# Last stage of a chained retention, hard-swish and SoLU kernel: word copies on ScalarE, the first pair's sums moved to the preceding block, output units within the last pair

## The chip, the cores and the metric

The kernel runs on one core of a Trainium2 chip. The metric is the device time of one execution in microseconds. Engines: TensorE (PE, with PEld for its weight loads), VectorE (DVE), ScalarE (ACT), GpSimd (POOL), and SyncE (SP), whose queue issues nearly all DMA transfers.

## The reference

```python
ret = (scale * q @ k.T * Dmat) @ v                 # 4 x 8 heads, 576 positions, 64 wide
x   = ret, heads side by side                      # 2304 tokens x 512
h   = x @ w_in                                     # 512 -> 2048
x   = (h * clip(h + 3, 0, 6) / 6) @ w_out          # 2048 -> 512: "x2" below
h   = x @ w_in2                                    # 512 -> 1024
e   = exp(h - max(h)); sm = e / (sum(e) + 1e-9)
s   = h * sm                                       # SoLU
ln  = (s - mean(s)) / sqrt(var(s) + 1e-6) * g_ln
out = ln @ w_out2                                  # 1024 -> 512
```

All in float32. The kernel keeps that accuracy by holding each matrix as two parts, a rounded one and the rest ("split": ScalarE copies the rounded part, GpSimd or VectorE subtracts it), and multiplying three times: high by high, high by low, low by high.

## The kernel before

The 2304 tokens are five blocks, four of 512 and block 4 of 256. A first stage computes the retention and, for the first six feed-forward groups of 128, a part of x2. Stage B goes over the blocks in the order `B_ORDER` = 3, 0, 1, 2, 4 and does the other ten groups: a first layer (`mlp_hs`: 40 steps of three matmuls each, four to a group; after each group ScalarE r, VectorE gf, ScalarE g, GpSimd g) and a second layer (`mlp_x2s`: 40 steps), whose sums `evac_full` adds to the earlier part and stores in DRAM as `x2f`. Beside stage B the second network's weights are prepared in 16 steps (`w2q`; ScalarE three activations each, VectorE, stores `w2s`), at the steps that `STEPS_B` lists for blocks 0, 1 and 2; their raw parts come by SP into two buffers `wraw`.

The last stage goes over nine pairs of 128-token tiles in the order `C_ORDER`, two pairs to a block of 512. The first product is a Strassen form: `load_x2` fetches a pair's x2 (`x2r`), `forms_x2` makes four sums on GpSimd and splits four operands into `xt` tiles (`his` on ScalarE, `los` on GpSimd), and `product` does seven products p = 0 to 6, each six matmuls, of prepared weight forms `w2t` (named b11, b21, t2, t1, b22, t3, t4 in that order). They are written in the groups (0,1), (2,3), (4,5), (6); a group's two banks are of a ring of two, so product 4 waits until the banks of products 0 and 1 have been read, product 6 until those of 2 and 3.

For each of the two tiles r of a pair VectorE then sums (`total`, `add_u`) with ScalarE's `first_u`, ScalarE takes `exp`, VectorE multiplies (`weigh`), ScalarE squares (`square`), GpSimd takes the power of the variance (`power`), VectorE normalizes (`norm`). The result must be transposed for the next product. The DMA engines transpose only 2-byte words, so `half_out` copies the lower (w = 0) and upper (w = 1) 16-bit words of each float apart into `lh`, an SP transfer transposes each into `lhT`, and `half_in` puts them together again in `lT` (w = 0 on VectorE, w = 1 on ScalarE). `split_hi` (ScalarE) and `split_lo` (GpSimd) make the two parts `lt` in a ring of four half tiles. `mm_out` is the output product: eight units of three matmuls for a tile, then ScalarE copies `osb` and SP stores it.

The order within each engine of the last stage is written out by hand. `at(when, fn)` notes an instruction with a planned time, `fill(n_small, n_out)` puts n_small steps of block 4's second layer (planned 0.36 us each) and n_out output units (0.68 us each) between the groups of products, and everything is emitted in order of planned time to engines that keep the order of the program. So a planned time only says which instruction stands behind which. Stage B isn't pinned in that way, save its weight steps; there a planner orders by its own costs. Output units begin in pair 2, four after each group; the last pair has none, and the remaining 56 follow it in one run. In pairs 0 and 1 the steps of block 4's second layer take their place.

Before block 4, pairs 0 and 1 (of block 2, the block just finished) are loaded; pair 0's forms are made inside block 4's first layer:

```python
load_x2(0)
load_x2(1)
...
for i, _ in enumerate(mlp_hs(t, FB, g4, g_4)):
    if i == 6:
        for step in chain(*forms_x2(0)):
            step()
```

Of the kernel before, what the change touches and what calls it, by code (L numbers as in the profile page):

```python
# [10 lines left out]
F32R = mybir.dt.float32r  # L11
# [3 lines left out]
ACTF = mybir.ActivationFunctionType  # L15
# [15 lines left out]
RELOAD = (0, 1, 2)  # L31
X2_LAG = 3
B_ORDER = (3, 0, 1, 2, 4)
C_ORDER = (2, 3, 0, 1, 4)
NX = 8
STEPS_B = ((6, 20, 42, 50, 58, 66), (6, 20, 42, 50, 58, 66), (6, 20, 42, 50))
W_FROM = 2
A_FROM = 4
AHEAD = 2
# [33 lines left out]
def retention_hardswish_solu_kernel(ctx, tc, kt, qt, kn, vt, w1, w2i, w2o, gln, decay, place, out):  # L73
# [580 lines left out]
    for i, _ in enumerate(first_b):  # L654
# [2 lines left out]
        j = i - NP * (len(FB) - X2_LAG)  # L657
        if 0 <= j < NP:
            xb[B_ORDER[1], j] = load_x(B_ORDER[1], j)
    w2q = Weights(w2_halves(pb), True)  # L660
    w2q.load_to(2)
    for k, t in enumerate(B_ORDER[1:-1]):
        after = B_ORDER[k + 2]
        for i, _ in enumerate(part_b(t)):
            if i in STEPS_B[k]:
                w2q.step()
            j = i - (4 * len(FB) + 4)
            if after in RELOAD and j >= 0 and j % 4 == 0 and j < 4 * NP:
                xb[after, j // 4] = load_x(after, j // 4)


    pairs = [(t, c) for t in C_ORDER for c in range(BLOCKS[t][1] // 256)]
    tiles = [BLOCKS[t][0] + 256 * c + 128 * i for t, c in pairs for i in range(2)]
    last = len(pairs) - 1
    xt = [p0.tile([128, 2, 512], F32R, tag="x", bufs=NX, name=f"xt{k}") for k in range(NX)]
    x2r, x2w, h2, ebuf, stats, us, lnT, turned, lTs = {}, {}, {}, {}, {}, {}, {}, {}, {}
    banks, raw_bufs = {}, []

    def load_x2(i):

# [11 lines left out]
    def forms_x2(i):  # L692

        lo, hi = x2r.pop(i)
        (a11, a21), (a12, a22) = (
            [x.rearrange("p k (t c) -> p t k c", c=128)[:, t] for t in range(2)] for x in (lo, hi)
        )
        s12, s34 = (pb.tile([128, 2, 2, 128], F32, tag="xraw", bufs=2, name=f"{n}_{i}") for n in ("s12", "s34"))
        xa = xt[6].rearrange("p a (i k c) -> p a i k c", i=2, k=2)[:, :, i % 2]
        x2, x12, x34 = xt[3 * (i % 2):3 * (i % 2) + 3]  # L700
        sums = [
            lambda o=o, a=a, b=b, op=op: ge.tensor_tensor(out=o, in0=a, in1=b, op=op) for o, a, b, op in (
                (s12[:, 0], a21, a22, ALU.add), (s12[:, 1], s12[:, 0], a11, ALU.subtract),
                (s34[:, 0], a11, a21, ALU.subtract), (s34[:, 1], a12, s12[:, 1], ALU.subtract),
            )
        ]
        splits = (
            (xa[:, 0], xa[:, 1], a11), (x2[:, 0], x2[:, 1], hi.rearrange("p k n -> p (k n)")),
            (x12[:, 0], x12[:, 1], s12.rearrange("p s k c -> p (s k c)")),
            (x34[:, 0], x34[:, 1], s34.rearrange("p s k c -> p (s k c)")),  # L710
        )
        his = [lambda a=a, v=v: se.activation(out=a, in_=v, func=ACTF.Copy) for a, _, v in splits]
        los = [
            lambda a=a, b=b, v=v: ge.tensor_tensor(out=b, in0=v, in1=f32(a), op=ALU.subtract) for a, b, v in splits
        ]
        x2w[i] = {
            name: [[x[:, a, at + k * step:at + k * step + 128] for a in range(2)] for k in range(2)]
            for name, x, at, step in (
                ("a11", xt[6], 256 * (i % 2), 128), ("a12", x2, 0, 256), ("a22", x2, 128, 256),
                ("s1", x12, 0, 128), ("s2", x12, 256, 128), ("s3", x34, 0, 128), ("s4", x34, 256, 128),  # L720
            )
        }
        return sums, his, los

    def product(i, p):

# [72 lines left out]
    def half_out(i, r, w):  # L799

        words = ebuf[i, r].rearrange("p a b -> p (a b)").bitcast(U16).rearrange("p (n w) -> p w n", w=2)
        if w == 0:
            turned[i, r] = p0.tile([128, 2, 8, 128], U16, tag="wraw", bufs=WRAW, name=f"lhT{i}_{r}")
        part = p0.tile([128, 1024], U16, tag=("wz", "wt")[w], bufs=2, name=f"lh{i}_{r}_{w}")
        ve.tensor_copy(out=part, in_=words[:, w])
        sy.dma_start(out=turned[i, r][:, w], in_=part, transpose=True)

    def half_in(i, r, w):
# [38 lines left out]
    t = B_ORDER[-1]  # L847
    load_x2p(t, 0)
    load_x2p(t, 1)
    load_x2(0)  # L850
    load_x2(1)
    g4, held = {}, []

    def g_4(ff):
# [5 lines left out]

    to_load = {18: ("b11", "wbi"), 22: ("b21", "wbi"), 28: ("t2", "wi"), 36: ("t1", "wi")}
    for i, _ in enumerate(mlp_hs(t, FB, g4, g_4)):
        if i == 6:
            for step in chain(*forms_x2(0)):
                step()
        if i in to_load:
            w2_load(*to_load[i])

# [39 lines left out]
    for i in range(last + 1):  # L908
        starts.append(now)
        for group in GROUPS:  # L910
            for p in group:
                at(now, product, i, p)
                now += 2 * UNIT
                ends[i, p] = now
            fill(5 if i == 0 else 4, 4 if 2 <= i < last else 0)
    fill(0, out_left)

    def spread(i, n, offsets):
# [8 lines left out]

    for i in range(last + 1):
        e = [ends[i, p] for p in range(7)]
        for when, fn, *args in (  # L930
            (e[0] + 0.2, first_u), (e[1] + 0.6, total, 0, 0, 2, 1), (e[2] + 0.1, add_u, 2, 2),
            (e[3] + 0.1, add_u, 4, 3), (e[4] + 0.1, total, 0, 1, 4, 4), (e[4] + 0.8, top, 0), (e[4] + 1.0, exp, 0),
# [7 lines left out]
            (e[4] + 16.8, split_hi, 0, 0), (e[4] + 17.4, split_hi, 0, 1),  # L940
            (e[4] + 17.5, split_lo, 0, 0), (e[4] + 18.8, split_lo, 0, 1),
            (e[6] + 14.0, half_in, 1, 0), (e[6] + 14.1, half_in, 1, 1),
            (e[6] + 23.5, split_hi, 1, 0), (e[6] + 24.1, split_hi, 1, 1),
            (e[6] + 24.2, split_lo, 1, 0), (e[6] + 25.5, split_lo, 1, 1),
        ):
            at(when, fn, i, *args)
        if i + 2 <= last:
# [62 lines left out]
```

## Time and profile before

| | us |
|---|---|
| runs shown (3) | 675.83, 678.3, 679.1 |
| median | 678.3 |
| the profiled execution | 678.33 |
| its span, first to last instruction | 676.5 |

| engine | busy us | share of the span | instructions |
|---|---|---|---|
| TensorE | 657.2 | 97% | 3914 |
| VectorE | 350.2 | 52% | 606 |
| ScalarE | 357.2 | 53% | 651 |
| GpSimd | 329.8 | 49% | 342 |

The shares are means over stages with different limits: VectorE's 52% is below 30% in some stretches and near 90% in the last stage. A matmul's end is modelled in the trace, so a busy TensorE may hide short pauses; the starts of runs of matmuls tell more. Planned engines keep their order, so an instruction can be late because the one ahead of it waits.

### The profile page before, as it was taken

The numbers are of one execution on the slowest core, as the hardware profiler recorded it, in microseconds if no ns is written. First come the engines' busy times: TensorE is split into PE (matmuls) and PEld (weight loads), VectorE is DVE, ScalarE is ACT, GpSimd is POOL, SyncE is SP. The second block draws the span as 40 slices with busy tenths as digits, with TensorE's granted clock in tenths as the row PEclk, the third lists the DMA queues.
The fourth block names the chain that finished last, engine by engine and source line by source line (L and its number), as shares of the span: only waits on it lengthen the run. The fifth ranks groups of instructions, "written<-read, shape, count | busy, mean of one in ns | idle before, by whom it ended". The sixth has DMA issues, their size and how long they took to land.

```text
span 676.5 us, 10633 instructions
## 1 busy us (share of the span) xinstructions
PE 657.2 (97%) x3914; PEld 545.0 (81%) x3914; DVE 350.2 (52%) x606; ACT 357.2 (53%) x651; POOL 329.8 (49%) x342
## 2 busy tenths in 40 slices
PE   9989999999999999999999999999999999999797
PEld 6778888887889888888888888898878777777587
DVE  1645445217213454244474344122888798889760
ACT  5878846346425665264364255043565665655453
POOL 4676744024222434145043033048796998888353
PEclk9999999999999999999999999999999999999799
DMA  9979727158206162558854732479683443343332
GB/s 319 303 257 329 262 72 240 47 165 324 88 32 187 50 200 84 156 167 284 321 171 157 247 126 78 140 268 354 129 230 91 97 111 81 96 104 78 79 73 83
DMA packets 80312, 112.92 MB, mean 167 GB/s; under 512 B 42626, under 2 KB 48002, under 8 KB 80260
## 3 DMA queue, kind: packets, MB, share of 16 engines
q1 hardware_dynamic: 80112, 112.22, 52.9%
q8 instruction: 31, 0.51, 0.3%
q14 instruction: 21, 0.17, 0.1%
q10 hardware_dynamic: 148, 0.01, 0.0%
HBM read 70.80 MB, written 31.98 MB: 152 GB/s over the span
## 4 chain that ended last, share of the span: by engine, by line
PE 65%; DVE 10%; POOL 7%; DMA 7%; ACT 6%; issue 4%; SPq 0%; ACTq 0%; POOLq 0%; DVEq 0%
PE h L260 25%; PE x L283 17%; PE acc L283 8%; PE o L69 5%; PE h L69 3%; DVE h L69 3%; PE xp L385 3%; POOL lt L69 2%; DVE lh L69 2%; ACT e L69 2%; DMA wraw<-in_w_dram 2%; POOL stat L69 2%; PE s L385 1%; PE x L69 1%; DVE e L69 1%
## 5 line engine op out<-in xcount | busy, mean ns | idle before, releaser
L277 POOL TENSOR_TENSOR g<-gf,g 128x512 fp32r<-128x512 f32 (+1 forms) x78 | 95.6, 1227 | 225.6 <-ACT g L276 215.9
L283 PE MATMUL x<-g,w 128*128 128x512 f32 x576 | 132.4, 389 | 0.1
L260 PE MATMUL h<-xb,w 128*128 128x512 f32 (+1 forms) x600 | 129.5, 359 | 1.0 <-DVE gf L271 1.0
L283 PEld LDWEIGHTS x<-g,w 128*128 128x128 f32 x576 | 108.0, 188 | 23.3 <-POOL g L277 0.5
L271 DVE SCALAR_TENSOR_TENSOR gf<-r,h 128x512 f32<-128x512 f32 (+1 forms) x80 | 50.6, 633 | 130.9 <-ACT r L270 105.5
L260 PEld LDWEIGHTS h<-xb,w 128*128 128x128 f32 x600 | 98.6, 189 | 17.1 <-DVE gf L271 1.2
L69 PE MATMUL o<-w,lt 128*128 128x512 f32 (+1 forms) x456 | 102.9, 378 | 1.6 <-DMA w<-w2s 1.6
L69 PEld LDWEIGHTS o<-w,lt 128*128 128x128 f32 x456 | 82.3, 188 | 18.4 <-DMA w<-w2s 2.4
L270 ACT ACTIVATE r<-h,half 128x512 f32<-128x512 f32 (+1 forms) x80 | 50.8, 638 | 61.6 <-PE h L260 61.5
L260 PE MATMUL h<-xB,w 128*128 128x512 f32 x360 | 82.4, 389 | 0.0
L260 PEld LDWEIGHTS h<-xB,w 128*128 128x128 f32 x360 | 67.6, 188 | 14.0
L69 POOL TENSOR_TENSOR lt<-lT,lt 128x512 fp32r<-128x512 f32 x36 | 58.4, 1639 | 22.6 <-ACT lt L69 12.2
L276 ACT ACTIVATE g<-gf 128x512 fp32r<-128x512 f32 (+1 forms) x78 | 46.0, 590 | 43.8 <-DVE gf L271 42.2
L69 ACT ACTIVATE e<-h,stat 128x1024 f32<-128x1024 f32 x36 | 41.2, 1145 | 39.4 <-DVE stat L69 39.4
L283 PE MATMUL acc<-g,w 128*128 128x512 f32 (+1 forms) x264 | 61.8, 360 | 0.0
L69 PE MATMUL h<-w2t,xt 128*128 128x512 f32 x216 | 55.5, 401 | 2.9 <-DVE h L69 2.9
L283 PEld LDWEIGHTS acc<-g,w 128*128 128x128 f32 x264 | 46.9, 188 | 8.7
L69 PEld LDWEIGHTS h<-w2t,xt 128*128 128x128 f32 x216 | 41.0, 193 | 13.6 <-DVE h L69 5.0
L141 DVE TENSOR_SCALAR wz<-wz 128x512 int32<-128x512 int32 x44 | 28.5, 649 | 40.0 <-ACT wz L133 39.9
L69 PE MATMUL h<-w2b,xt 128*128 128x512 f32 x162 | 41.7, 403 | 4.6 <-DVE stat L69 4.4
L69 DVE COPY lh<-e 128x1024 uint16<-128x1024 uint16 x36 | 42.8, 1211 | 0.2
L69 PEld LDWEIGHTS h<-w2b,xt 128*128 128x128 f32 x162 | 30.5, 193 | 12.7 <-DVE stat L69 6.7
(113 smaller groups left out, 850.8 us busy)
## 6 DMA issues: line engine op xcount, KB each, us to landing
wraw<-in_w_dram SPq DMA_DIRECT2D x32, 512.0 KB, 5.0
xs<-xb SPq DMA_DIRECT2D x12, 512.0 KB, 5.9
xB<-xs SPq DMA_DIRECT2D x12, 512.0 KB, 6.5
rv<-in_vt_dram SPq DMA_DIRECT2D x16, 288.0 KB, 5.7
x2l<-x2s SPq DMA_DIRECT2D x18, 256.0 KB, 4.0
x2r<-x2f SPq DMA_DIRECT2D x9, 512.0 KB, 4.4
out_dram<-osb SPq DMA_DIRECT2D x17, 256.0 KB, 2.1
x2s<-x2p SPq DMA_DIRECT2D x16, 256.0 KB, 2.7
```

The costliest lines, as they stand in the source:

```text
L69: return lambda *args, **kw: self.keep(op(*args, **kw))
L141: ve.tensor_scalar(out=z, in0=z, scalar1=3, scalar2=None, op0=ALU.logical_shift_left)
L260: nc.tensor.matmul(hp, w1t[ff, 0][:, a, c], xb[t, p][:, b, :n], start=(p == 0 and i == 0), stop=(p == NP - 1 and i == 2),)
L270: se.activation(out=r, in_=hp, func=ACTF.Relu, scale=1.0 / 6.0, bias=half)
L271: ve.scalar_tensor_tensor(out=gf, in0=r, scalar=1.0, in1=hp, op0=ALU.min, op1=ALU.mult)
L276: se.activation(out=g[ff][:, 0], in_=gf, func=ACTF.Copy)
L277: ge.tensor_tensor(out=g[ff][:, 1], in0=gf, in1=f32(g[ff][:, 0]), op=ALU.subtract)
L283: te.matmul(acc, w1t[ff, 1][:, a, c], g[:, b], start=(first and i == 0), stop=(last and i == 2))
L385: keep(nc.tensor.matmul(*args, **kw))
```

## The change

Five edits, all for the last stage or just ahead of it.

1. `C_ORDER` begins with block 3, whose x2 is stored long before. The loads of pairs 0 and 1 and pair 0's `forms_x2` go into `before_c`, called at steps 41, 42 and 52 of block 2's stage B (1, 2 and 12 of its second layer). The `xt` tiles are taken there, and renumbered so that pair 0's lie in slots that were block 1's.
2. The four weight steps of block 2 go from its steps 6, 20, 42, 50 to 4, 12, 20, 28, all in the first layer.
3. `half_out` copies the upper words on ScalarE instead of VectorE.
4. Two output units follow each group of the last pair.
5. The last tile's splits are planned 18.0 us after the pair's last product instead of 23.5.

```diff
@@ -31,9 +31,9 @@
 RELOAD = (0, 1, 2)
 X2_LAG = 3
 B_ORDER = (3, 0, 1, 2, 4)
-C_ORDER = (2, 3, 0, 1, 4)
+C_ORDER = (3, 0, 1, 2, 4)
 NX = 8
-STEPS_B = ((6, 20, 42, 50, 58, 66), (6, 20, 42, 50, 58, 66), (6, 20, 42, 50))
+STEPS_B = ((6, 20, 42, 50, 58, 66), (6, 20, 42, 50, 58, 66), (4, 12, 20, 28))
 W_FROM = 2
 A_FROM = 4
 AHEAD = 2
@@ -657,24 +657,11 @@
         j = i - NP * (len(FB) - X2_LAG)
         if 0 <= j < NP:
             xb[B_ORDER[1], j] = load_x(B_ORDER[1], j)
-    w2q = Weights(w2_halves(pb), True)
-    w2q.load_to(2)
-    for k, t in enumerate(B_ORDER[1:-1]):
-        after = B_ORDER[k + 2]
-        for i, _ in enumerate(part_b(t)):
-            if i in STEPS_B[k]:
-                w2q.step()
-            j = i - (4 * len(FB) + 4)
-            if after in RELOAD and j >= 0 and j % 4 == 0 and j < 4 * NP:
-                xb[after, j // 4] = load_x(after, j // 4)
-
-
     pairs = [(t, c) for t in C_ORDER for c in range(BLOCKS[t][1] // 256)]
     tiles = [BLOCKS[t][0] + 256 * c + 128 * i for t, c in pairs for i in range(2)]
     last = len(pairs) - 1
-    xt = [p0.tile([128, 2, 512], F32R, tag="x", bufs=NX, name=f"xt{k}") for k in range(NX)]
     x2r, x2w, h2, ebuf, stats, us, lnT, turned, lTs = {}, {}, {}, {}, {}, {}, {}, {}, {}
-    banks, raw_bufs = {}, []
+    banks, raw_bufs, xt = {}, [], []
 
     def load_x2(i):
 
@@ -696,8 +683,8 @@
             [x.rearrange("p k (t c) -> p t k c", c=128)[:, t] for t in range(2)] for x in (lo, hi)
         )
         s12, s34 = (pb.tile([128, 2, 2, 128], F32, tag="xraw", bufs=2, name=f"{n}_{i}") for n in ("s12", "s34"))
-        xa = xt[6].rearrange("p a (i k c) -> p a i k c", i=2, k=2)[:, :, i % 2]
-        x2, x12, x34 = xt[3 * (i % 2):3 * (i % 2) + 3]
+        xa = xt[3].rearrange("p a (i k c) -> p a i k c", i=2, k=2)[:, :, i % 2]
+        x2, x12, x34 = xt[4 * (i % 2):4 * (i % 2) + 3]
         sums = [
             lambda o=o, a=a, b=b, op=op: ge.tensor_tensor(out=o, in0=a, in1=b, op=op) for o, a, b, op in (
                 (s12[:, 0], a21, a22, ALU.add), (s12[:, 1], s12[:, 0], a11, ALU.subtract),
@@ -716,11 +703,36 @@
         x2w[i] = {
             name: [[x[:, a, at + k * step:at + k * step + 128] for a in range(2)] for k in range(2)]
             for name, x, at, step in (
-                ("a11", xt[6], 256 * (i % 2), 128), ("a12", x2, 0, 256), ("a22", x2, 128, 256),
+                ("a11", xt[3], 256 * (i % 2), 128), ("a12", x2, 0, 256), ("a22", x2, 128, 256),
                 ("s1", x12, 0, 128), ("s2", x12, 256, 128), ("s3", x34, 0, 128), ("s4", x34, 256, 128),
             )
         }
         return sums, his, los
+
+    def before_c(i):
+
+        if i == 1:
+            xt.extend(p0.tile([128, 2, 512], F32R, tag="x", bufs=NX, name=f"xt{k}") for k in range(NX))
+            load_x2(0)
+        elif i == 2:
+            load_x2(1)
+        elif i == 12:
+            for step in chain(*forms_x2(0)):
+                step()
+
+    w2q = Weights(w2_halves(pb), True)
+    w2q.load_to(2)
+    for k, t in enumerate(B_ORDER[1:-1]):
+        after = B_ORDER[k + 2]
+        for i, _ in enumerate(part_b(t)):
+            if i in STEPS_B[k]:
+                w2q.step()
+            if t == B_ORDER[-2]:
+                before_c(i - 4 * len(FB))
+            j = i - (4 * len(FB) + 4)
+            if after in RELOAD and j >= 0 and j % 4 == 0 and j < 4 * NP:
+                xb[after, j // 4] = load_x(after, j // 4)
+
 
     def product(i, p):
 
@@ -802,7 +814,10 @@
         if w == 0:
             turned[i, r] = p0.tile([128, 2, 8, 128], U16, tag="wraw", bufs=WRAW, name=f"lhT{i}_{r}")
         part = p0.tile([128, 1024], U16, tag=("wz", "wt")[w], bufs=2, name=f"lh{i}_{r}_{w}")
-        ve.tensor_copy(out=part, in_=words[:, w])
+        if w:
+            se.activation(out=part, in_=words[:, w], func=ACTF.Copy)
+        else:
+            ve.tensor_copy(out=part, in_=words[:, w])
         sy.dma_start(out=turned[i, r][:, w], in_=part, transpose=True)
 
     def half_in(i, r, w):
@@ -847,8 +862,6 @@
     t = B_ORDER[-1]
     load_x2p(t, 0)
     load_x2p(t, 1)
-    load_x2(0)
-    load_x2(1)
     g4, held = {}, []
 
     def g_4(ff):
@@ -860,9 +873,6 @@
 
     to_load = {18: ("b11", "wbi"), 22: ("b21", "wbi"), 28: ("t2", "wi"), 36: ("t1", "wi")}
     for i, _ in enumerate(mlp_hs(t, FB, g4, g_4)):
-        if i == 6:
-            for step in chain(*forms_x2(0)):
-                step()
         if i in to_load:
             w2_load(*to_load[i])
 
@@ -912,7 +922,7 @@
                 at(now, product, i, p)
                 now += 2 * UNIT
                 ends[i, p] = now
-            fill(5 if i == 0 else 4, 4 if 2 <= i < last else 0)
+            fill(5 if i == 0 else 4, 0 if i < 2 else 4 if i < last else 2)
     fill(0, out_left)
 
     def spread(i, n, offsets):
@@ -927,6 +937,7 @@
 
     for i in range(last + 1):
         e = [ends[i, p] for p in range(7)]
+        late = e[6] + (23.5 if i < last else 18.0)
         for when, fn, *args in (
             (e[0] + 0.2, first_u), (e[1] + 0.6, total, 0, 0, 2, 1), (e[2] + 0.1, add_u, 2, 2),
             (e[3] + 0.1, add_u, 4, 3), (e[4] + 0.1, total, 0, 1, 4, 4), (e[4] + 0.8, top, 0), (e[4] + 1.0, exp, 0),
@@ -940,8 +951,8 @@
             (e[4] + 16.8, split_hi, 0, 0), (e[4] + 17.4, split_hi, 0, 1),
             (e[4] + 17.5, split_lo, 0, 0), (e[4] + 18.8, split_lo, 0, 1),
             (e[6] + 14.0, half_in, 1, 0), (e[6] + 14.1, half_in, 1, 1),
-            (e[6] + 23.5, split_hi, 1, 0), (e[6] + 24.1, split_hi, 1, 1),
-            (e[6] + 24.2, split_lo, 1, 0), (e[6] + 25.5, split_lo, 1, 1),
+            (late, split_hi, 1, 0), (late + 0.6, split_hi, 1, 1),
+            (late + 0.7, split_lo, 1, 0), (late + 2.0, split_lo, 1, 1),
         ):
             at(when, fn, i, *args)
         if i + 2 <= last:
```

## Rows read from the trace of the kernel before

**Rows 1.** Busy us of each engine by stretch (x instructions), granted clock, DMA

```profile
388.00:415.00 27.00, 27.00 (x121) 22.36 (x120) 11.67 (x16) 14.88 (x24) 10.71 (x9) 1.00 0.36 121
...
415.00:442.30 27.30, 27.30 (x123) 22.62 (x122) 6.96 (x10) 5.01 (x8) 2.27 (x2) 1.00 0.31 97
...
583.94:605.47 21.53, 21.00 (x92) 16.75 (x91) 19.23 (x31) 12.88 (x23) 18.65 (x19) 1.00 0.41 98
...
627.03:640.05 13.02, 8.59 (x26) 6.52 (x25) 10.62 (x20) 4.79 (x10) 4.87 (x5) 0.74 0.49 102
```

**Rows 2.** Chain that ended last, in order of time: start, us, tile

```profile
387.89 27.20 PE h L260 x120
...
530.83 3.13 DMA lhT<-lh
```

**Rows 3.** TensorE, block 4 and pairs 0 to 3: start, us, operation, tiles

```profile
442.13 13.11 PE L260 MATMUL h<-xb,w 128*128 128x256 f32 x108
...
460.34 2.91 PE L69 MATMUL h<-w2b,xt 128*128 128x512 f32 x12
...
515.09 2.88 PE L69 MATMUL h<-w2b,xt 128*128 128x512 f32 x12
```

**Rows 4.** TensorE from pair 6 on [idle <-releaser]

```profile
597.16 1.65 PE L69 MATMUL h<-w2t,xt 128*128 128x512 f32 x6 [0.48 <-DVE h L69]
...
622.91 2.89 PE L69 MATMUL h<-w2b,xt 128*128 128x512 f32 x12
...
632.99 2.93 PE L69 MATMUL h<-w2b,xt 128*128 128x512 f32 x6 [4.43 <-DVE stat L69]
...
639.89 33.14 PE L69 MATMUL o<-w,lt 128*128 128x512 f32 x168
```

**Rows 5.** GpSimd (POOL) in block 4's first layer and in a steady pair

```profile
453.72 1.30 POOL L714 TENSOR_TENSOR xt<-x2r,xt 128x512 fp32r<-128x512 f32 x1
...
585.76 3.97 POOL L69 TENSOR_TENSOR lt<-lT,lt 128x512 fp32r<-128x512 f32 x2
...
599.35 2.55 POOL L69 TENSOR_TENSOR lt<-lT,lt 128x512 fp32r<-128x512 f32 x2
```

**Rows 6.** VectorE (DVE) in a steady pair and at the end

```profile
588.62 1.66 DVE L69 COPY lh<-e 128x1024 uint16<-128x1024 uint16 x1
...
592.52 2.26 DVE L69 COPY lh<-e 128x1024 uint16<-128x1024 uint16 x2
...
634.63 0.69 DVE L69 COPY lh<-e 128x1024 uint16<-128x1024 uint16 x1
...
641.93 1.22 DVE L69 SCALAR_TENSOR_TENSOR h<-h,e 128x1024 f32<-128x1024 f32 x1
```

**Rows 7.** Waits of TensorE from 440 us on: total us, times, longest

```profile
PE o L69 <- DMA w<-w2s: 1.6, 2, 1.2
...
PE h L260 <- DVE gf L271: 1.0, 1, 1.0
...
PE x L69 <- DVE gf L271: 0.9, 1, 0.9
```

**Rows 8.** The queue of SyncE (SP): DMA issues in order of time

```profile
498.27 1.09 SPq L69 DMA_DIRECT2D w<-w2s  x2
```

**Rows 9.** Groups of ScalarE, 540.87 to 605.47 us: busy, mean ns | idle

```profile
L69 ACT ACTIVATE e<-h,stat 128x1024 f32<-128x1024 f32 x13 | 14.9, 1144 | 12.4 <-DVE stat L69 12.4
...
L69 ACT ACTIVATE lT<-lhT 128x1024 uint16<-128x1024 uint16 x6 | 8.3, 1376 | 0.0
...
L69 ACT ACTIVATE lt<-lT 128x512 fp32r<-128x512 f32 x12 | 6.9, 621 | 4.9 <-DVE lT L69 4.9
```

**Rows 10.** ScalarE (ACT) in a steady pair and in the last pair

```profile
593.11 0.64 ACT L69 ACTIVATE xt<-s 128x512 fp32r<-128x512 f32 x1 [2.87 <-POOL s L69]
...
630.42 0.58 ACT L69 ACTIVATE h<-h 128x512 f32<-128x512 f32 x1
...
645.55 0.63 ACT L69 ACTIVATE lt<-lT 128x512 fp32r<-128x512 f32 x1 [2.03 <-PE o L69]
```

## The prediction

> **What bounds the kernel now.** I read the busy time by stretch first, to see which engine sets the time in which stage. Up to the end of block 2 TensorE has no gap: its two layers take 27 us each with ScalarE, VectorE and GpSimd far from full [rows 1]. The chain that ended last gives the price of one 512-column matmul there: 27.20 us / 120 = 0.2267 us [rows 2]. A steady pair of the last stage needs 42 of these for its products and 48 for its 16 output units: 90 x 0.2267 = 20.40 us. It takes more: pair 3 begins at 515.09 [rows 3] and pair 8, the last, at S = 622.91 [rows 4], so five pairs take 107.82 us, 21.56 each. The missing 1.16 us are short pauses ahead of products 4 and 6 behind VectorE, as the 0.48 us at 597.16 and the slow refill behind it [rows 4].
>
> The other engines' rows of a steady pair say why: VectorE is busy 19.23 of 21.53 us, GpSimd 18.65, ScalarE only 12.88 [rows 1]. The chain in order of time runs in that stage through GpSimd, VectorE and ScalarE and never through TensorE. Its round, from one split of output words to the next: GpSimd's two subtractions (585.76, 3.97 us) [rows 5], the power of the row's variance, VectorE's norm, its two copies of words (592.52, 2.26) [rows 6], an addition, a word put back, then ScalarE's splits, its own word, exp, VectorE's weighing, ScalarE's square, GpSimd again. So the pairs are bound by a round of queues of about 21.5 us, with TensorE 1.16 us below it.
>
> Outside the steady pairs TensorE waits in three places. In block 4's first layer and its first accumulation it stands 1.0 and 0.9 us [rows 7], because GpSimd has the sums and splits of pair 0's x2 in front of block 4's g (one is at 453.72) [rows 5]. In pair 2 it waits 1.6 us, in two parts, for the last output weights [rows 7], whose transfers SP issues only at 498.27 [rows 8]. In the last pair, which has no output units between its products, it waits 4.43 us ahead of product 4 [rows 4], and the granted clock of that stretch is 0.74 in the mean [rows 1]: the engine had stood still, and the next matmuls ran at 1.2 instead of 2.4 GHz. From S the products and the 168 matmuls left end at 639.89 + 33.14 = 673.03 = S + 50.1; the work is 42 x 0.2267 + 33.1 = 42.6, so 7.5 us are lost there, 4.4 by waiting and 3.1 by the clock.
>
> **The change part by part.**
>
> *Pair 0 first from block 3.* Its load and its twelve sums and splits go to block 2's second layer, where ScalarE is busy 5.01 and GpSimd 2.27 of 27.3 us and TensorE doesn't wait for either [rows 1]; the slots of xt0 to xt3 were block 1's. Hidden there at no cost; were the cover gone, the 1.9 us of block 4 would come back. In block 4 GpSimd then has only g. From 442.13 to 460.34 TensorE does 132 matmuls of 256 columns; at 13.11 / 108 = 0.1214 each that is 16.0 instead of 18.2 us. **Gain 2.2** (at least the two waits, 1.9; if the planner puts the forms back beside block 4, nothing). Two x2r loads leave SP's burst at block 4's start for block 2's second layer, behind nothing there that waits (block 3's x2 was stored two blocks before); no matmul waits for that burst, so I count nothing.
>
> *The last weight steps earlier.* Two of four steps go from the second to the first layer of block 2. A step has three ScalarE activations, about as long as a split of 621 ns [rows 9], so 4 us more beside 14.88 of 27.0 [rows 1], with their two raw loads and two stores on SP in the same 27 us. TensorE has four banks ahead of ScalarE. At no cost; uncovered it would be those 4 us.
>
> *Upper words by ScalarE.* Two copies per pair leave VectorE: 1.66 us (row 0) and half of 2.26 (row 1), 2.8 together, because each collides with GpSimd; the same copy alone takes 0.69 [rows 6]. ScalarE's copy isn't in the trace, but the way back is, same size and with the stride on the other side: 1376 ns [rows 9]. I take 1.38 (from 2 x 0.62, twice a split of half the elements, to 1.38). ScalarE goes to 12.9 + 2.8 = 15.6 of 20.4. What is queued behind: row 0's copy stands ahead of the next pair's splits of x2 and fits into the 2.87 us that ScalarE idles before 593.11 [rows 10]. Row 1's stands right behind that split and ahead of row 0's word on its way back: it ends at 593.11 + 0.64 + 1.38 = 595.1, VectorE's second copy ended at 592.52 + 2.26 = 594.8. The transfer that waits for it takes 3.13 us [rows 2], and exp stands behind the word that it brings. On this path the move gains nothing by itself.
>
> What shortens the round is GpSimd: the pair of subtractions takes 3.97 us beside both copies and 2.55 beside none [rows 5]. One copy of two goes, and the two tiny power steps behind it lose their collision too: I take 0.9 (bounds 0 and 1.42). That split of x2 and all that follows it come as much earlier, so the round is 21.53 - 0.9 = 20.6, just above TensorE's 20.40 (bounds 20.4 and 21.5). **Gain over five pairs 5 x 0.96 = 4.8** (0.3 to 5.8).
>
> By the Trainium skill, SBUF — State Buffer, section "Who interferes with whom", a copy of VectorE in its two-port mode holds the ports that GpSimd shares for its whole length and the other one blocks; a removed copy would then free GpSimd for its own 0.69 us only, the round would be 20.8, and the five pairs would give 3.6. The trace's 3.97 against 2.55 agrees: 1.42 is two such lengths.
>
> *Pair 2.* VectorE has lost two copies by then (row 0's and row 1's of pair 0), at least 2 x 0.69, and block 4's last sums, whose stores stand ahead of the weights' transfers on SP, come that much earlier. Pair 2 took 515.09 - 492.50 = 22.6 us (its start worked out from [rows 3]: 460.34 and 84 x 0.2267 + 108 x 0.1214 us of matmuls without a wait); 1.6 of it is the wait for weights. **Gain 1.0** (0 to 2.2).
>
> *Output units within the last pair.* Two after each group move 24 matmuls, 5.4 us, into the pair. Product 4 needs ScalarE's first copy of the pair (ends 630.42 + 0.58 = S + 8.1) [rows 10] and one VectorE sum, 0.7 us: ready at S + 8.8, since the copy of words that stood between them is gone. TensorE arrives at 24 x 0.2267 + 4 units x 0.68 = S + 8.2. So 0.6 us of the 4.43 stay, too short to expect the low clock: after the longer part of pair 2's wait, 1.2 us [rows 7], the products of pair 3 still took 2.88 us for twelve [rows 3]. What is late next: on ScalarE the split for tile 14's second half waits until tile 12 has been used (as at 645.55 [rows 10]), and tile 12 is now used up only at the pair's end, T = S + 15.6. Queued behind it, from T: that split 0.6, exp 1.14, a word 1.38, square 1.14, an output 0.5, exp 1.14, VectorE's weighing 1.2 [rows 6], square 1.14, the new word copy 1.38, an output 0.5, tile 15's split 0.6 [rows 9], in all 10.7, and GpSimd's subtraction 1.3: T + 12.0. TensorE reaches tile 15 at T + 16 x 0.68 = T + 10.9. A wait of 1.2 (bounds 0 and 3). After it tiles 16 and 17 find their splits done, one to two us ahead. **Gain 7.5 - 0.6 - 1.2 = 5.7** (1.5 with a fall of the clock, 7.5 with no wait). The earlier time of the last splits, 18.0 instead of 23.5 after the last product, keeps them between the outputs of tiles 15 and 16 in ScalarE's order, where they were: no cost, no gain; behind tile 16's output they would hold up tile 17.
>
> Sum: 2.2 + 1.0 + 4.8 + 5.7 = 13.7 us. The profiled execution took 678.33 us (span 676.5 and 1.8 around it), which is the median of the runs shown, 678.3. 678.3 - 13.7 = **664.6 us**.
>
> **The rivals.**
>
> *ScalarE takes the round over.* The word copy of row 1, its transfer and the word back are ahead of exp, and there ScalarE gains nothing over VectorE. If GpSimd gets no faster, the round is 21.3: 2.2 + 0.5 + 1.3 + 5.7 = 9.7, 668.6 us. For it: nothing gained on that path itself. Against it: 2.55 beside 3.97. Chance 0.22.
> A rule speaks for this side: ScalarE: Activation LUTs of the Trainium skill, section "Rules for kernel authors", gives simple elementwise work to VectorE rather than ScalarE, as VectorE is faster per element. The trace's undisturbed copy agrees, 0.69 against 1.38, but the copies in this stage are the disturbed ones.
>
> *The last pair still loses its clock.* Product 4 comes 1.7 us late (4.43 less the four units' 2.7, VectorE's saving lost), and with tile 15's wait the clock falls, 3.1 more: the tail gives 1.5 and the time is 668.8 us. For it: 0.74 in the old stretch. Against: the copy in front of the sum is gone. Chance 0.12.
>
> *Every wait goes.* 2.2 + 2.2 + 5.8 + 7.5 = 17.7: 660.6 us. Against it: the list on ScalarE behind tile 12. Chance 0.10.
>
> *The forms don't leave block 4* (that part isn't pinned): 666.8 us. Chance 0.04.
>
> *Slower: the round gets longer.* If row 1's word copy comes late on ScalarE, its transfer and exp come late in every pair. Start, pair 2 and tail give 8.9, so this decides only above 21.56 + 8.9 / 5 = 23.3 us per pair, 1.8 us late on each copy; at 24 us the time is 681.6. Against it: ScalarE has 2.87 us idle right before. Chance 0.04.
>
> **How the numbers follow.** The forecast has the rest, 0.48, and by its own terms 661.5 to 667.5. For 8 in 10 the range takes in the rivals at 668.6 and 668.8 with some of their bounds, and goes down to nearly no wait at all: 660.7 to 670.4. About 0.5%, 3.4 us, is what a measurement can tell here (the three runs lie between 675.83 and 679.1). All cases but the last are faster by more; 0.03 of them I put within that bound, where several terms lie at their low ends: faster 0.93, same 0.03, slower 0.04.
>
> **What would show it.** Right: no wait of TensorE in block 4's first layer; starts of pairs 3 to 8 about 20.6 us apart; GpSimd's pair of subtractions near 3.1 us; VectorE below 17 us per pair, ScalarE near 15.6; the wait ahead of the last pair's product 4 under 1 us and the clock at 1.00; a wait of about 1 us at tile 15. Wrong: a copy of words on ScalarE well over 1.4 us, pairs still at 21.5 with exp waiting for the word back, a low clock after S, or a new wait of TensorE in block 2's layers.

## The result, and the profile after

The changed kernel took 670.32 us in the median of its first four runs (669.1 to 671.65), the kernel before 677.86: a ratio of 0.9892, 95% interval 0.9857 to 0.9927. Run again beside other kernels it took 668.13 us, the kernel before 678.21: 0.9852, 0.9826 to 0.9878. So it is faster, by 7.5 and by 10.1 us (1.1 and 1.5%), where 13.7 were forecast. The table cuts the profiled executions at the same instructions; each piece is a difference of two starts of matmuls, the last one ends with the last output matmul.

| us | before | after | difference | forecast |
|---|---|---|---|---|
| up to block 4's first matmul | 442.13 | 442.97 | +0.84 | 0 |
| block 4 to product 0 of pair 0 | 18.21 | 15.83 | -2.38 | -2.2 |
| pairs 0 and 1 | 32.16 | 32.16 | 0 | 0 |
| pair 2 | 22.59 | 22.53 | -0.06 | -1.0 |
| pairs 3 to 7 | 107.82 | 105.42 | -2.40 | -4.8 |
| last pair and outputs | 50.12 | 45.26 | -4.86 | -5.7 |
| all from block 4 on | 230.90 | 221.20 | -9.70 | -13.7 |

Nothing is changed in the first 440 us, and yet block 4's first matmul lies between 440.6 and 443.1 us in the profiles of this study, the kernel before's included. From block 4 on the pieces of the changed kernel repeat within a tenth of a us, all but the last one, where the clock fell in some executions; so these pieces are what is compared below.

TensorE of the changed kernel, in order of time, answers to [rows 3, 4]:

```profile
442.97 14.55 PE L260 MATMUL h<-xb,w 128*128 128x256 f32 x120
...
457.36 1.60 PE L69 MATMUL x<-g,w 128*128 128x256 f32 x12
...
501.85 0.96 PE L69 MATMUL o<-w,lt 128*128 128x512 f32 x3 [1.18 <-DMA w<-w2s]
...
534.79 3.00 PE L69 MATMUL h<-w2b,xt 128*128 128x512 f32 x12 [0.74 <-DVE h L69]
...
555.51 2.97 PE L69 MATMUL h<-w2b,xt 128*128 128x512 f32 x12
...
576.22 3.00 PE L69 MATMUL h<-w2b,xt 128*128 128x512 f32 x12
...
618.91 2.97 PE L69 MATMUL h<-w2b,xt 128*128 128x512 f32 x12 [1.28 <-ACT e L69]
...
627.43 1.66 PE L69 MATMUL h<-w2b,xt 128*128 128x512 f32 x6
...
645.86 0.73 PE L69 MATMUL o<-w,lt 128*128 128x512 f32 x2 [0.38 <-ACT lt L69]
...
647.66 16.51 PE L69 MATMUL o<-w,lt 128*128 128x512 f32 x94 [1.07 <-POOL lt L69]
```

Block 4's two waits are gone: 120 and 12 matmuls run through from 442.97 to 458.8. The wait for the last output weights in pair 2 is as before. The wait ahead of product 6 in each pair is gone, but there is a new one ahead of product 0 of the next pair, 0.74 us at pair 4, about 0.2 us at pairs 5 to 7 (from start to start those pairs are 20.7 us, 0.3 above TensorE's own 20.40), and 1.28 us at the last pair. In the last pair product 4 starts nearly without a pause (4.43 us before), and in the output run behind it tile 15 is waited for in two pieces, 0.38 and 1.07 us.

Busy time by stretch (columns as in [rows 1]): block 4's start, pair 5, the last pair.

```profile
442.97:458.80 15.83, 15.83 (x133) 15.83 (x132) 4.90 (x11) 8.57 (x20) 6.67 (x9) 1.00 0.84 296
...
555.51:576.22 20.71, 20.68 (x90) 16.82 (x91) 15.72 (x29) 14.88 (x24) 17.83 (x19) 1.00 0.42 101
...
618.91:633.07 14.16, 14.05 (x60) 11.26 (x61) 11.18 (x26) 9.64 (x14) 5.67 (x10) 1.00 0.38 81
```

In a steady pair VectorE is busy 15.7 instead of 19.2 us, ScalarE 14.9 instead of 12.9, GpSimd 17.8 instead of 18.65. The last pair has its full clock. Three engines' rows of pair 6, GpSimd, VectorE and ScalarE, answer to [rows 5, 6, 10] (the last row of VectorE is of pair 7, the last one of ScalarE of the last pair):

```profile
583.07 3.98 POOL L69 TENSOR_TENSOR lt<-lT,lt 128x512 fp32r<-128x512 f32 x2
...
587.01 0.46 POOL L69 TENSOR_TENSOR stat<-stat 128x1 f32<-128x1 f32 x2
...
595.84 2.55 POOL L69 TENSOR_TENSOR lt<-lT,lt 128x512 fp32r<-128x512 f32 x2
```

```profile
582.43 1.76 DVE L69 SCALAR_TENSOR_TENSOR h<-h,e 128x1024 f32<-128x1024 f32 x1
...
584.30 1.60 DVE L69 COPY lh<-e 128x1024 uint16<-128x1024 uint16 x1
...
589.39 1.11 DVE L69 COPY lh<-e 128x1024 uint16<-128x1024 uint16 x1
...
593.78 1.00 DVE L69 COPY lT<-lhT 128x1024 uint16<-128x1024 uint16 x1 [1.43 <-DMA lhT<-lh]
...
595.51 0.68 DVE L69 CUSTOM_DVE_ANT_0 h<-h,h 128x512 f32<-128x512 f32 x1
...
597.53 1.94 DVE L69 SCALAR_TENSOR_TENSOR h<-h,e 128x1024 f32<-128x1024 f32 x1 [0.73 <-ACT e L69]
...
615.00 1.74 DVE L69 COPY lT<-lhT 128x1024 uint16<-128x1024 uint16 x1 [1.95 <-DMA lhT<-lh]
```

```profile
590.53 1.04 ACT L69 ACTIVATE lh<-e 128x1024 uint16<-128x1024 uint16 x1
...
595.03 1.39 ACT L69 ACTIVATE lT<-lhT 128x1024 uint16<-128x1024 uint16 x1 [0.52 <-DMA lhT<-lh]
...
596.28 1.13 ACT L69 ACTIVATE e<-h,stat 128x1024 f32<-128x1024 f32 x1
...
634.64 0.63 ACT L69 ACTIVATE lt<-lT 128x512 fp32r<-128x512 f32 x1 [1.75 <-PE o L69]
```

GpSimd's pair of subtractions (583.07) takes 3.98 us, as before, and still runs beside VectorE's weighing of a row (582.43) and one copy of words (584.30); the two small steps behind it take 0.46 instead of 0.91. The copy of words on ScalarE takes 1.04 us, where 1.38 was taken. Before the words of row 1 on their way back VectorE and ScalarE now stand idle for the transfer, 1.43 and 0.52 us, and behind VectorE's are the sums that free the next pair's banks, behind ScalarE's is exp.

### The profile page after: what moved, and what is told of

Read it like the earlier page. It is cut to its first block, busy times and chain, and to the rows that moved or that the text cites. A ratio compares the mean times of both kernels' runs of the same rounds, so it can differ in the third digit from the quotient of the medians.

```text
span 667.4 us, 10625 instructions
## 1 busy us (share of the span) xinstructions
PE 653.4 (98%) x3914; PEld 543.3 (81%) x3914; DVE 327.5 (49%) x588; ACT 374.8 (56%) x669; POOL 323.0 (48%) x342
## 4 chain that ended last, share of the span: by engine, by line
PE 76%; DMA 6%; DVE 5%; ACT 5%; POOL 5%; issue 3%; SPq 0%; POOLq 0%; ACTq 0%; DVEq 0%
PE h L260 26%; PE x L283 18%; PE h L69 8%; PE o L69 8%; PE acc L283 8%; DMA rq<-in_qt_dram 3%; PE xp L385 2%; PE x L69 2%; DVE h L69 2%; PE s L385 2%; ACT e L69 2%; POOL lt L69 1%; POOL stat L69 1%; DMA wraw<-in_w_dram 1%; DMA lhT<-lh 1%
## 5 line engine op out<-in xcount | busy, mean ns | idle before, releaser
L69 PE MATMUL h<-w2t,xt 128*128 128x512 f32 x216 | 53.5, 390 | 0.0
L251 POOL TENSOR_TENSOR xb<-xa,xb 128x512 fp32r<-128x512 f32 (+7 forms) x32 | 27.5, 879 | 24.0 <-ACT xb L250 24.0
L133 ACT ACTIVATE wz<-wraw 128x512 f32<-128x512 f32 x44 | 28.9, 658 | 17.6 <-DMA wraw<-in_w2o_dram 9.1
```

Of the source, the lines that this page charges most:

```text
L69: return lambda *args, **kw: self.keep(op(*args, **kw))
L133: first = se.activation(out=z.bitcast(F32), in_=raw[:, :, 1].bitcast(F32), func=ACTF.Prelu, scale=2.0 ** -112, alpha=2.0 ** 32)
L251: ge.tensor_tensor(out=x[:, 1, c], in0=src, in1=f32(x[:, 0, c]), op=ALU.subtract)
```

## The experiments

**The three parts alone.** Words on ScalarE only:

```diff
-        ve.tensor_copy(out=part, in_=words[:, w])
+        if w:
+            se.activation(out=part, in_=words[:, w], func=ACTF.Copy)
+        else:
+            ve.tensor_copy(out=part, in_=words[:, w])
```

> The kernel before with only the upper words moved to ScalarE. If the shorter round of queues is what this edit gives, pairs 4 to 6 begin 20.7 us apart instead of 21.55, as in the changed kernel, and five pairs give about 3 us; ahead of the last pair's product 4 TensorE waits about 1.6 us less than 4.43. Expected: 4 to 6 us faster than before, some 673 us. If instead ScalarE's queue takes the round over without the other edits, pairs stay at 21.3 or more and the gain is under 2 us.

Measured: 672.58 us, ratio 0.9925 (0.9911 to 0.9938), 5.4 us. From start to start, pairs 3 to 7 took 20.40, 20.40, 20.46, 20.71 and 21.96 us. TensorE's rows from pair 7 on:

```profile
598.22 3.00 PE L69 MATMUL h<-w2b,xt 128*128 128x512 f32 x12
...
620.18 2.97 PE L69 MATMUL h<-w2b,xt 128*128 128x512 f32 x12 [1.28 <-ACT e L69]
...
628.71 2.15 PE L69 MATMUL h<-w2b,xt 128*128 128x512 f32 x6 [2.84 <-DVE stat L69]
```

The first pairs run at TensorE's own 20.40 us, pair 6 at 20.7, and the last pair starts 1.28 us late. Pair 2 took 24.17 us here, since the weights were waited for 3.1 us. A reading that fits: TensorE began pair 3 late, with the other queues ahead of it, and they lost that lead at some 0.3 us a pair until they were behind again. Pairs 2 to 7 together took 128.1 us, and 127.95 in the changed kernel: a wait of TensorE for weights in pair 2 costs nothing as long as the queues need that time anyway.

The order alone (edits 1 and 2):

> Only the first pair from block 3, its sums in block 2's second layer, and the four earlier weight steps. If block 4's waits are all that this is worth, the stretch from block 4's first matmul to product 0 of pair 0 is 15.8 instead of 18.2 us, the rest stays, and the time falls by 2.4 us, to about 675.5. If the head start is given back later, at pair 2's wait for the weights, no gain.

Measured: 674.36 us, 0.9948 (0.9934 to 0.9963), 3.6 us. From block 4's first matmul to product 0 of pair 0 it takes 15.83 us, 2.38 less; pair 2 takes 0.66 more, pairs 3 to 7 0.85 less. The last pair waits as long as before:

```profile
628.90 2.49 PE L69 MATMUL h<-w2b,xt 128*128 128x512 f32 x6 [4.44 <-DVE stat L69]
```

Even so, that pair and the outputs take 49.01 us, 1.11 less than before, since the clock fell less: 0.90 in the mean of the pair's first 17.2 us, and 0.80 in the kernel before. So 2.4 us of the gain are block 4's, as expected; most of the rest is a difference of the clock that the edits don't explain.

The units alone (edits 4 and 5):

> Only the two output units after each group of the last pair and the earlier last splits. If the units alone cover the wait, the wait ahead of the last pair's product 4 falls from 4.43 to 1.7 us and the clock stays high: 4 to 5 us faster, about 673. If the copy of words on VectorE in front of the sum is needed out of the way too, the clock still falls after the wait and the gain is about 1.5 us, 676.

Measured: 674.37 us, 0.9951 (0.9932 to 0.997), 3.6 us. The last pair and its outputs take 47.42 us instead of 50.12:

```profile
634.99 1.74 PE L69 MATMUL h<-w2b,xt 128*128 128x512 f32 x6 [1.81 <-DVE stat L69]
...
655.49 16.79 PE L69 MATMUL o<-w,lt 128*128 128x512 f32 x94 [0.43 <-POOL lt L69]
```

The wait ahead of product 4 is 1.81 us, where 1.7 were worked out, and the mean clock from 624 to 645 us is 0.92. So the units alone cover 2.6 us of the wait, as worked out, but the clock still fell behind the rest of it, and the gain lies between the two that were expected. This execution was the slowest of its six (677.3 us): in block 4, where nothing was changed, TensorE stood for two groups instead of one, 1.41 us more. In the words-only kernel, with the copy out of the way and no units, 2.84 us of the wait ahead of product 4 stay.

The three parts give 5.4, 3.6 and 3.6 us alone and 7.5 to 10.1 together. The wait ahead of product 4 adds up: 1.59 us less by the words, 2.62 by the units, 4.16 by all edits. The time of the last pair and its outputs does not: 2.65 us less by the words, 1.11 by the order, 2.70 by the units, and 4.86 by all. In each of the three profiles a part of the clock's loss is already gone, which can be won back only once, and with all edits a pause at tile 15 appears, 1.45 us, of which the kernels with one part show none or 0.43.

**What holds the pairs at 20.72 us.** Row 1's words on the way back, later in the order written by hand: VectorE's behind the next pair's sums, ScalarE's behind its exp.

```diff
-        if w == 0:
+        if (i, r) not in lTs:
...
-            (e[6] + 14.0, half_in, 1, 0), (e[6] + 14.1, half_in, 1, 1),
+            (e[6] + 17.2, half_in, 1, 0), (e[6] + 16.2, half_in, 1, 1),
```

The first two lines only let whichever word comes first take the tile.

> The changed kernel, with row 1's two words put back later in the hand-written order: on VectorE behind the next pair's sums of products 4 and 5, on ScalarE behind its exp. Theory A: the changed kernel's pairs are held at 20.72 us by VectorE and ScalarE standing still for the transfer of row 1's words (1.4 and 0.5 us per pair). Then pairs fall to 20.4 to 20.5 us, the 1.28 us ahead of the last pair's product 0 and the 0.74 us ahead of pair 4's go, and the time is about 3 us below the changed kernel's. Theory B: the collisions of VectorE and GpSimd hold the round. Then pairs stay at 20.7 us and the time is the changed kernel's.

Measured: 663.75 us, 0.979 (0.9775 to 0.9805): 14.2 us less than before. The five pairs take 20.40 us each, and neither pair 4 nor the last one starts late. Theory A holds, and the gain is more than the 3 us that it gave: from block 4 on 217.0 us, 4.2 less than in the changed kernel. Each of the two words alone:

> The changed kernel with only VectorE's word of row 1 put back later (behind the next pair's sums); ScalarE's stays ahead of exp. If VectorE's standing still ahead of the sums is what stops TensorE at the next pair's product 0, the pairs fall to 20.4 us with this alone. If exp behind ScalarE's word sets the round, they stay above 20.6 us.

Measured: 667.08 us, 0.9832 (0.981 to 0.9854). Pairs 4 to 7 take 20.7 to 21.0 us, and the last pair's product 4 waits 1.75 us.

> The changed kernel with only ScalarE's word of row 1 put back later (behind the next pair's exp); VectorE's stays ahead of the sums. If exp behind ScalarE's word sets the round, pairs fall to 20.4 to 20.5 us with this alone; if VectorE's word does, they stay at 20.7 us and the 1.28 us ahead of the last pair's product 0 stay too.

Measured: 663.62 us, 0.9795 (0.9764 to 0.9825). Pairs 5 to 7 take 20.40 us, 3 and 4 take 20.5, and the last starts on time. So it is ScalarE's word ahead of exp that sets the round. VectorE's stays ahead of the sums in this run, and the later pairs still take TensorE's own 20.40 us. ScalarE's rows there:

```profile
589.20 1.15 ACT L69 ACTIVATE e<-h,stat 128x1024 f32<-128x1024 f32 x1 [1.11 <-DVE stat L69]
...
590.34 1.36 ACT L69 ACTIVATE lT<-lhT 128x1024 uint16<-128x1024 uint16 x1
```

exp now waits for VectorE's sums (1.11 us) and no longer for the word, which comes after it without a wait.

**Whether the copies set GpSimd's time.** Row 0's lower words are copied on ScalarE too, in the changed kernel (`if w or r == 0`), so that no copy of VectorE runs beside GpSimd's pair of subtractions:

> The changed kernel with row 0's lower words taken apart by ScalarE too, so that VectorE has no copy beside GpSimd's pair of subtractions of the row before. In the changed kernel that pair still takes 3.98 us, as before. If the copy that is left beside it is why, the pair falls to about 3 us, the power behind it comes that much earlier, and the round gets shorter than TensorE's 20.4 us: pairs 20.4 us, up to 2 us less in all. If VectorE's weighing collides with it as well, the pair stays above 3.5 us and the round gains under 0.3 us.

Measured: 666.54 us, 0.983 (0.981 to 0.985). The pair of subtractions with no copy beside it, on GpSimd, and the weighing on VectorE that still is:

```profile
580.70 3.53 POOL L69 TENSOR_TENSOR lt<-lT,lt 128x512 fp32r<-128x512 f32 x2
...
584.20 0.45 POOL L69 TENSOR_TENSOR stat<-stat 128x1 f32<-128x1 f32 x2
```

```profile
580.07 1.76 DVE L69 SCALAR_TENSOR_TENSOR h<-h,e 128x1024 f32<-128x1024 f32 x1
```

It takes 3.53 us, half of the shortening that was expected. Of the 1.43 us that the changed kernel's pair has above the 2.55 of the pair beside neither weighing nor copy, the copy accounts for 0.45; for the 0.98 that are left the only long instruction of VectorE beside it is the weighing, itself 1.76 us long instead of 1.22. The power comes 0.45 us earlier. Pairs 3 to 7 take 20.40 us each, pairs 2 to 7 together 126.9 instead of 127.95. Whether the round itself is now below 20.40 us this run doesn't show: the weights were waited for longer (2.47 us), the clock fell behind that wait (0.72 in the mean of 500.5 to 506.6 us), and pair 2 took 24.89, so TensorE began pair 3 late and the queues had a lead, as with the words alone.

**Pair 2's weights.** With both words later, the last weights requested ahead of block 4's last four sums:

```diff
-                if k == end and d % 2 == 1:
-                    for dd in (d - 1, d):
-                        evac_full(t, dd, accs[d // 2][:, dd % 2])
                 if d == NP - 1 and k % 2 == 1 and k != 3:
                     w2_load(max(0, k // 2 - 1), "wbo" if k == 1 else "wo")
+                if k == end and d == NP - 1:
+                    for dd in range(NP):
+                        evac_full(t, dd, accs[dd // 2][:, dd % 2])
```

> The kernel with both words put back later, and in addition block 4's four last sums and stores put behind the request for the last output weights, so that SP doesn't stand behind VectorE's sums before it issues it. If pair 2's wait for the weights is a late issue, the issue moves from 3.9 us after the last x2 matmul to about 1 us after it, the 1.5 us of waiting go, and pair 2 takes 20.4 to 21 us: 1.5 us below the kernel with the words later. If the transfers themselves are too long beside the others, the wait stays.

Measured: 664.8 us, 0.9814 (0.9776 to 0.9852), no gain over the words later alone. The request goes out at once (487.31; at 496.70 in the changed kernel), and TensorE doesn't wait for the weights. But pair 2 takes 23.64 us. SP's row, then the waits of 480 to 515 us:

```profile
487.31 2.09 SPq L69 DMA_DIRECT2D w<-w2s  x2
```

```profile
DVE x2o L69 <- DMA x2f<-x2o: 4.8, 1, 4.8
...
PE o L69 <- POOL lt L69: 2.1, 1, 2.1
```

The four sums share two buffers; the stores that free them now stand behind the request for the weights on SP, VectorE stands 4.8 us in front of the third sum, and a tile's part comes 2.1 us late. So the sums were written two to a buffer, with one store for two:

> The kernel with both words put back later, the last weights requested ahead of block 4's last sums, and these sums written two to a buffer, so that VectorE doesn't stand 4.8 us for a store to free one of the two buffers, as it did when the weights went first. If that standing is what made tile parts late in pair 2, then neither the weights nor the parts are waited for: pair 2 takes 20.4 to 21 us, 1.5 us less than with the words later alone. If the parts are late for another reason, the wait for them stays.

Measured: 662.16 us, 0.9761 (0.9737 to 0.9785). Pair 2 takes 21.30 us with 0.56 us of wait for a tile's part: 1.26 us less than with the words later alone, and in the median of runs the difference to it (1.6 us, measured in another batch) is about the scatter.

**Tile 15.** With both words later, the last pair's units as 4, 4, 0, 0:

```diff
-            fill(5 if i == 0 else 4, 0 if i < 2 else 4 if i < last else 2)
+            fill(5 if i == 0 else 4, 0 if i < 2 else 4 if i < last or group[0] < 4 else 0)
```

> The kernel with both words put back later, and the last pair's eight output units as 4, 4, 0, 0 after its groups instead of 2, 2, 2, 2. If tile 15 comes late because ScalarE stands in front of exp until tile 12 has been used, then tile 12 is now used up ahead of product 4, the list starts some 2 us earlier, and the wait of 1.3 us at tile 15 goes, with the low clock that it brings in some executions: 1 to 2 us below the kernel with the words later. If the list itself is the limit, the wait only moves.

Measured: 662.49 us, 0.9766 (0.9742 to 0.979). TensorE has no wait from the last pair's start to the end:

```profile
614.62 2.88 PE L69 MATMUL h<-w2b,xt 128*128 128x512 f32 x12
...
629.58 28.02 PE L69 MATMUL o<-w,lt 128*128 128x512 f32 x144
```

629.58 + 28.02 - 614.62 = 42.98 us for the last pair and its outputs, 44.47 with the words later alone and 42.6 by the matmuls.

**The changed kernel again**, for its scatter:

> The changed kernel as it is, once more, beside the other kernels of this batch. By the stages of its first profile (9.7 us less than before from block 4 on, 0.8 us more ahead of it, where nothing was changed) it should lie at 668 to 670 us; if the two executions at 671.5 us of four were the rule, at 671 or more, with a stretch of low clock that the first profile doesn't show.

Measured: 668.13 us (667.22 to 669.48). From block 4 on its pieces are those of the first profile within 0.1 us, but for the last one, 47.11 instead of 45.26. TensorE's rows at tile 15, and the stretch around them:

```profile
643.95 0.73 PE L69 MATMUL o<-w,lt 128*128 128x512 f32 x2 [0.66 <-ACT lt L69]
...
645.77 18.07 PE L69 MATMUL o<-w,lt 128*128 128x512 f32 x94 [1.08 <-POOL lt L69]
```

```profile
643.90:650.00 6.10, 4.96 (x14) 3.65 (x15) 2.40 (x3) 4.31 (x7) 4.40 (x3) 0.72 1.06 233
```

The wait for tile 15 was 1.74 us in this execution and 1.45 in the first, and after it the granted clock is 0.72 in the mean of 6 us: the low level, 1.2 GHz, for a part of them. The same 94 matmuls take 18.07 us instead of 16.51; with the 0.29 us of longer wait that is the 1.85 us. The executions of the changed kernel with a mean clock of 0.995 to 0.997 are the slower ones of each set (671.65, 671.32; 669.48, 668.77), those at 0.999 to 1.000 the faster (669.1, 669.32; 667.22, 667.49).

**All three together** (words later, weights first with two sums to a buffer, units 4, 4, 0, 0):

> The words put back later, the weights first with two sums to a buffer, and the units 4, 4, 0, 0. If the three waits are separate, the last stage has no wait of TensorE left from block 4 on: 15.8 + 32.2 + 6 x 20.4 + 42.9 = 213.3 us from block 4's first matmul on, against 221.2 in the changed kernel, and about 660 us in all. If they give way to one another, it stays near 663.

Measured: 660.39 us (660.01 to 661.33), 0.9743 (0.9723 to 0.9762), 17.1 us less than before. What TensorE waits for from 440 us on:

```profile
PE o L69 <- POOL lt L69: 0.8, 1, 0.8
```

That wait is in pair 2, which takes 21.49 us. From block 4 on it is 214.5 us, where 213.3 were worked out for no wait at all. In the same batch the two kernels with only the weights or only the units beside the later words took 662.16 and 662.49 us, so these two gains don't replace each other; how large each is within the sum these runs don't fix, as the units' profile had only 0.76 us of wait for weights in pair 2 and already 214.7 us from block 4 on.

## Why the prediction came out as it did

The direction held, the size didn't: 7.5 and 10.1 us instead of 13.7. By its own steps:

*Pair 0 first from block 3:* right. 2.38 us measured, 2.2 forecast, hidden in block 2's second layer at no cost, and the weight steps too: block 2's layers take 27.2 us each, as before.

*Upper words by ScalarE:* the step that failed is the gain over five pairs, 4.8 forecast and 2.40 measured, with pair 2's 1.0, of which 0.06 came. Three things in it were wrong.

First, the source. The two subtractions were to shorten by the copy's leaving, to near 3.1 us, and they stayed at 3.98. The rows of the kernel before, on VectorE and on GpSimd, show what else ran there:

```profile
585.12 1.76 DVE L69 SCALAR_TENSOR_TENSOR h<-h,e 128x1024 f32<-128x1024 f32 x1
...
586.99 1.59 DVE L69 COPY lh<-e 128x1024 uint16<-128x1024 uint16 x1
...
600.70 2.28 DVE L69 SCALAR_TENSOR_TENSOR h<-h,e 128x1024 f32<-128x1024 f32 x1 [0.40 <-ACT e L69]
```

```profile
589.69 0.91 POOL L69 TENSOR_TENSOR stat<-stat 128x1 f32<-128x1 f32 x2
```

The 3.97 us from 585.76 on [rows 5] lie beside the weighing (585.12) and the lower words' copy (586.99), which both stayed. The upper words' copy (588.62 [rows 6]), which left, overlapped with their last 1.1 us only. "Beside both copies" left the weighing out, and that 1.42 us are twice a copy's 0.69 was a coincidence: without any copy 0.98 us of the 1.43 stay. What got shorter was the power's two small steps, 0.46 for 0.91, and the weighing behind exp, 1.94 for 2.28 in the same place (1.22 undisturbed [rows 6]). Together these are 0.79 us, and the round fell from 21.53 to 20.72; no run takes the two apart. So the round came near the forecast 20.6 by another way than the one worked out, which was luck.

Second, the path on which "the move gains nothing by itself" was the path that set the round. Row 1's word, transfer and way back stand ahead of exp; with ScalarE's word out of the way the later pairs took 20.40 us. The first rival named this place, but gave the whole round 21.3 us; only pair 3 took that, the others 20.72.

Third, the two ends of the five pairs were left out, and pair 2 was added as a term of its own. Against five times 20.6 us, pair 3 with 21.30 loses 0.7 us, pairs 4 to 6 lose 0.36, and pair 7 with 21.96, the late last start in it, loses 1.36: that is the missing 2.4. Ahead of the last start VectorE's word came back 3.8 us after its copy had ended (3.3 a pair earlier), and the copy into place (615.00) took 1.74 us beside GpSimd. Both ends go when ScalarE's word is put behind exp (20.5 and 20.40 us). And pair 2 is no term of its own: pairs 2 to 7 take 128 us together whether TensorE waits 1.5 or 3.1 us for weights in pair 2. The queues, not TensorE, decide when the last pair begins.

(The lock rule of the Trainium skill, SBUF — State Buffer, section "Who interferes with whom", had given a round of 20.8 by shortening the subtractions by one copy's length; the round came near it, but not in that way.)

*Pair 2:* VectorE's two copies less hardly brought the last sums forward. SP's row shows the request at 496.70, 1.57 us earlier than in [rows 8], just as much as TensorE itself is earlier:

```profile
496.70 1.10 SPq L69 DMA_DIRECT2D w<-w2s  x2
```

VectorE's saving ended in waits, among them 0.60 us for a product of TensorE and 0.32 for exp; the third sum then stood 1.71 us until a store had freed a buffer (1.53 before):

```profile
486.91 0.69 DVE L69 CUSTOM_DVE_ANT_0 h<-h,h 128x512 f32<-128x512 f32 x1 [0.60 <-PE h L69]
...
495.36 0.76 DVE L69 TENSOR_TENSOR x2o<-x,x2l 128x256 f32<-128x256 f32 x2 [1.71 <-DMA x2f<-x2o]
```

That the late request is what TensorE waits for is shown by the request put first: the wait for weights goes, but the sums' two buffers then hold up VectorE.

*Output units within the last pair:* 4.86 of 5.7. Product 4 came in time (0.6 forecast, about 0.3 of pause measured). The list on ScalarE behind tile 12 was right item for item: tile 12 used up at T = 634.4, the wait of ScalarE's split at 634.64, tile 15's subtraction done 13.2 us after T where 12.0 were worked out, a pause of 1.9 us, with the slower matmuls between its two waits, where 1.2 were. With both words later, the units moved ahead of product 4 take it away. The fall of the clock, priced in the term's bounds and in a rival, came behind this pause in some executions: in the two profiles 1.6 us lie between the run of 94 matmuls with it and without it.

The first runs lie at the range's upper edge (670.32 against 670.4) and outside it if their ratio is laid on 678.3 (671.0); the second set, 668.1, lies inside. Every wait gone was priced at 660.6; the kernel with the three waits removed took 660.4. That this is so near is in part luck: from block 4 on it gains 16.4 us, not 17.7, and 1.2 us come from the start of block 4, where nothing was changed.

What stays open is why the start of block 4 differs by 2.5 us from execution to execution, and when the clock falls. The length of the wait alone doesn't decide it. It fell after 1.74 us at tile 15 (the changed kernel again), 1.81 ahead of product 4 (units alone) and 2.47 in pair 2 (row 0's words). It stayed at 1.00 after 1.75 ahead of product 4 (VectorE's word later), 1.76 at tile 15 (row 0's words) and 2.71 in pair 2 (words alone). The rows of pair 2 with words alone, then with row 0's words, with three and six matmuls behind the wait:

```profile
504.50 0.96 PE L69 MATMUL o<-w,lt 128*128 128x512 f32 x3 [2.71 <-DMA w<-w2s]
```

```profile
500.89 3.02 PE L69 MATMUL o<-w,lt 128*128 128x512 f32 x6 [2.47 <-DMA w<-w2s]
```

## What to carry to other kernels

When work is moved off a busy engine, follow what comes back from it: the moved copy's result returned through a transfer to a place ahead of exp in a fixed order, and putting that word behind exp gave 4.5 us more than the change itself, in the same batch. Terms of one chain can't be added per stage: ask which queue decides when the next stage starts, and count a wait of another engine before it as nothing until that queue is ahead. When two instructions overlap and both are long, look at everything that runs beside them before saying which one holds the other up. And a gain on a round that lies a few tenths above the main engine's own time is worth those tenths in each turn, and nothing beyond.

## What the runs showed that was not expected

ScalarE took 128x1024 16-bit words apart (stride on the reading side) in 1.04 us, and put them together (stride on the writing side) in 1.37. VectorE's weighing, two inputs of 128x1024 floats, took 1.22 us alone and 1.76 to 2.28 beside GpSimd. GpSimd's pair of subtractions took 2.55 us alone, 3.53 beside the weighing and 3.98 beside the weighing and a copy of words. TensorE's clock was granted at 0.72 in the mean of 6 us after waits of 1.74 and 2.47 us, and stayed at 1.00 after one of 2.71.
